# Start-up of a gated SSM and GELU-MLP kernel: warm-up matmuls on a constant, and one joint transpose of the state and bias rows behind the transposes of x

## The chip, the cores and the metric

The kernel runs on 1 core of one Trainium2 chip. The metric is the device time of one execution in microseconds (us). A run executes a kernel several times; the text quotes medians with the lowest and highest. The profile's span, from the first to the last instruction, is 1.7 to 2.2 us shorter than the time of the same execution.

## The reference, cut to what matters

```python
x = A_x                                     # 1 x 2048 x 640, bf16
g = sigmoid((x * gate_w).sum(-1))
a = S5 scan over 2048 steps: Bu = x @ B_bar.T ; h = Lam_bar * h + Bu ; y = 2 Re(h @ C.T) + x * Dskip
b = gelu(x @ w1 + b1) @ w2 + b2             # 640 -> 1728 -> 640
out = g * a + (1 - g) * b
```

`Lam_bar` and `B_bar` come from three vectors of 640 values (`Lambda_re`, `Lambda_im`, `log_dt`). For the argument only the beginning matters: the first 512 rows of x are transposed on TensorE, multiplied with W1 (five blocks of 128 input columns, k = 0 to 4, and seven column blocks of the output, jf = 0 to 6: 35 matmuls), and meanwhile the three state vectors and the bias b1, which arrive as rows, are transposed into columns.

## The kernel before

A small list scheduler, written in Python, orders the operations of each engine by priority and estimated duration when the program is built. Each engine then runs its own list in order, waiting on semaphores. `op(name, engine, duration, reads, writes, fn, prio)` is how an operation enters it.

```python
# loads: SP queue                                   (cut: B, C, W2, later x)
for h in range(2):                                  # first 512 rows of x in two halves, 320 KB each
    load(f"x0_{h}", "sp", ..., xn[0][:, 2 * h:2 * h + 2, :], x2[h * 256:(h + 1) * 256, :]..., prio=h)
for k in range(KD):                                 # W1, columns 0:896, 224 KB each
    load(f"w1_{k}", "sp", ..., W1sb[:, k, 0:FW], B_w1[k * 128:(k + 1) * 128, 0:FW], [("w1", k)], prio=2 + k)
# loads: ACT queue: three state vectors, the bias b1 in three pieces (behind a POOL memset of b1rows)

wz = SB("wz", [128, 512], BF16)                     # cleared by VectorE
def f_warm():
    for _ in range(6):
        t = nc.tensor.matmul(PS[6][:, :], wz[:, 0:128], wz[:, :], start=True, stop=True)
op("warm", "pe", 2.4, ["wz"], [("bank", 6)], f_warm, prio=-1000)

# TensorE, in the order in which the scheduler puts it:
#   six warm-ups | ten transposes of x, rows 0:256 | three transposes of the state rows ("cols")
#   | ten transposes of x, rows 256:512 | one filler matmul on wz | W1 matmuls k = 0, k = 1
#   | transpose of the bias rows ("colb") | W1 matmuls k = 2, 3, 4 | ...
# VectorE: copy of the state columns, five copies PSUM -> xT (k = 0..4), scan tables, ..., copy of the bias columns

for k in range(KD):                                 # first W1 matmuls, accumulating in banks 0 to 6
    for jf in ((5, 6, 0, 1, 2, 3, 4) if k == 0 else range(NW)):
        matmul(PS[jf], W1sb[:, k, jf * 128:(jf + 1) * 128], xT[:, k, 0:512], start=(k == 0), stop=(k == KD - 1))
```

The x transposes use banks 0 to 4, so W1 matmuls 5 and 6 can start as soon as xT block 0 is copied, and those of banks 0 to 4 need their bank's copy.

Of the kernel before, what the change touches and what calls it, by code (L numbers as in the profile page):

```python
# [8 lines left out]
FP32 = mybir.dt.float32  # L9
BF16 = mybir.dt.bfloat16  # L10
# [137 lines left out]
class Prog:  # L148
# [8 lines left out]
    def op(self, name, eng, dur, reads, writes, fn, prio=None, lat=0.0, after=()):  # L157
        deps = {}
        for k in reads:
            for w in self.last_w.get(k, ()):  # L160
                deps[w.idx] = w
        for k in writes:
            for w in self.last_w.get(k, ()):
                deps[w.idx] = w
            for r in self.last_r.get(k, ()):
                deps[r.idx] = r
        for a in after:
            deps[a.idx] = a
        deps = list(deps.values())
        E = self.E  # L170

        def run(eg, deps=deps, eng=eng, fn=fn):
            E.wait(eng, *[d.done for d in deps])
            return fn()

        it = self.sch.add(name, eng, dur, deps, run, prio=prio, lat=lat)
        for k in writes:
            self.last_w[k] = [it]
            self.last_r[k] = []
        for k in reads:  # L180
            self.last_r.setdefault(k, []).append(it)
        return it


def bass_gated_mix__ssm_conv_s5__dense_activation_gelu__prompt_kernel(
# [18 lines left out]
    _, S, D = A_x.shape  # L204
    P = A_Lambda_re.shape[0]
    F = B_w1.shape[1]
    assert S % 512 == 0 and D % 128 == 0 and P == D
    KD = D // 128
    KP = P // 128
# [4 lines left out]
    NF = (F + 127) // 128  # L214
    FL = F - (NF - 1) * 128
# [10 lines left out]
    with ExitStack() as es, nc.Block() as block:  # L226

        def SB(name, shape, dt):
            return es.enter_context(nc.sbuf_tensor(name, list(shape), dt))

        xT = SB("xT", [128, KD, S], BF16)
        xn = [SB(f"xn_{i}", [128, 4, D], BF16) for i in range(2)]
# [5 lines left out]
        GlL = [SB(f"GlL_{i}", [65, 512], BF16) for i in range(3)]  # L238
        dsk = SB("dsk", [128, D], BF16)
        gwb = SB("gwb", [128, D], BF16)  # L240
        b1col = SB("b1col", [128, NF], FP32)
        rows = SB("rows", [KP, 3, 128], BF16)
        b1rows = SB("b1rows", [NF, 128], BF16)
        lcol = SB("lcol", [128, 3, KP], FP32)
        dtb = SB("dtb", [128, KP], BF16)
        acol = SB("acol", [128, KP], FP32)
        thcol = SB("thcol", [128, KP], FP32)
# [5 lines left out]
        ident = SB("ident", [128, 128], BF16)  # L253
# [33 lines left out]
        PS = [es.enter_context(nc.psum_tensor(f"ps{i}", [128, 512], FP32)) for i in range(8)]  # L287
# [17 lines left out]
        op = pr.op  # L305

        def inc(eng, ins):
            return E.inc(eng, ins, eng + "_s")

        def dma_inc(eng, ins, sem):  # L310
            SEM(sem)
            E.count.setdefault(sem, 0)
            ins.then_inc(sems[sem], 16)
            E.count[sem] += 16
            return (sem, E.count[sem])
# [11 lines left out]
        def load(name, eng, sem, dst, src, writes, prio, dur=0.5, lat=2.5, reads=(), **kw):  # L327
            def fn():
                return dma_inc(eng, engines[eng].dma_start(dst, src), sem)
            return op(name, eng, dur, reads, writes, fn, prio=prio, lat=lat)  # L330
# [22 lines left out]
        load("w1_r", "sp", "l_w1r", W1sb[:, :, FW:F], B_w1[:, FW:F].rearrange("(k p) f -> p k f", p=128), [("w1", "r")], prio=6.5, lat=6.0)  # L353
        nmain = (NF - 1) * 128

        def f_b1z():
            return inc("pool", nc.gpsimd.memset(b1rows[:, :], 0.0))

        op("b1z", "pool", 0.2, (), ["b1a", ("b1b", 0), ("b1b", 1)], f_b1z, prio=-50)
        for i, (nm, src) in enumerate((("lre", A_Lambda_re), ("lim", A_Lambda_im), ("ldt", A_log_dt))):  # L360
            load(nm, "act", "l_" + nm, rows[:, i, :], src.rearrange("(k p) -> k p", p=128), [("rows", i)], prio=-100 + i, dur=0.45)
        load("b1a", "act", "l_b1a", b1rows[0:NF - 1, :], B_b1[0:nmain].rearrange("(j p) -> j p", p=128), ["b1a"], prio=-97, dur=0.4, lat=2.5)
        for h in range(2):
            load(f"b1b{h}", "act", f"l_b1b{h}", b1rows[NF - 1:NF, h * 64:h * 64 + FL], B_b1[nmain:F].rearrange("(j p) -> j p", j=1), [("b1b", h)],
                 prio=-96 + h, dur=0.4, lat=2.5)


# [12 lines left out]

        op("const", "dve", 0.8, ["iota"], ["ident"], f_const, prio=-65)

        wz = SB("wz", [128, 512], BF16)

        def f_wz():
            return inc("dve", nc.vector.memset(wz[:, :], 0.0))  # L386

        op("wz", "dve", 0.35, (), ["wz"], f_wz, prio=-70)

        def f_warm():  # L390
            t = None
            for _ in range(6):
                t = nc.tensor.matmul(PS[6][:, :], wz[:, 0:128], wz[:, :], start=True, stop=True)  # L393
            return inc("pe", t)

        op("warm", "pe", 2.4, ["wz"], [("bank", 6)], f_warm, prio=-1000)

        def f_ones():
            t = None
# [6 lines left out]
        def filler(name, n, prio, deps):  # L406
            def fn():
                t = None
                for _ in range(n):
                    t = nc.tensor.matmul(PS[6][:, :], wz[:, 0:128], wz[:, :], start=True, stop=True)  # L410
                return inc("pe", t)
            op(name, "pe", n * 0.22, ["wz"] + deps, [("bank", 6)], fn, prio=prio)

        for h in range(2):
            for k in range(KD):
# [6 lines left out]
                    return inc("pe", t)  # L422

                op(f"tp{h}{k}", "pe", 0.13, [("xn", 0, h), "ident"], [("bank", k)], f_tp, prio=-900 + 20 * h + k)
        filler("fill", 1, -860, [("xn", 0, 1)])
        for k in range(KD):

            def f_tpe(k=k):
# [7 lines left out]
        psC = PS[7][:, :].bitcast(BF16)  # L436

        def f_cols():
            t = None
            for i in range(3):  # L440
                t = nc.tensor.transpose(psC[:, i * 8:i * 8 + KP], rows[:, i, :], ident[0:KP, 0:KP])  # L441
            return inc("pe", t)

        op("cols", "pe", 0.3, [("rows", 0), ("rows", 1), ("rows", 2), "ident"], [("bank", 7)], f_cols, prio=-870)

        def f_cols1():
            return inc("dve", nc.vector.tensor_copy(out=lcol[:, :, :], in_=psC[:, 0:24].rearrange("p (a k) -> p a k", a=3)[:, :, 0:KP]))

        op("cols1", "dve", 0.2, [("bank", 7)], ["lcol"], f_cols1, prio=-3000)
        psD = PS[7][:, :].bitcast(BF16)  # L450

        def f_colb():
            return inc("pe", nc.tensor.transpose(psD[:, 0:NF], b1rows[:, :], ident[0:NF, 0:NF]))  # L453

        op("colb", "pe", 0.1, ["b1a", ("b1b", 0), ("b1b", 1), "ident"], [("bank", 7)], f_colb, prio=14.5)

        def f_colb1():
            return inc("dve", nc.vector.tensor_copy(out=b1col[:, :], in_=psD[:, 0:NF]))

        op("colb1", "dve", 0.2, [("bank", 7)], ["b1col"], f_colb1, prio=-1000)  # L460

        def f_dt():
            return inc("act", nc.scalar.activation(dtb[:, :], lcol[:, 2, :], ACT.Exp))

# [496 lines left out]
```

## Time and profile before

| | before |
|---|---|
| time, median of 3 (low to high) | 217.87 us (217.17 to 218.08) |
| span of the profiled run | 215.4 us |
| TensorE busy | 211.7 us, 98% |
| VectorE busy | 191.8 us, 89% |
| first W1 matmul | 6.10 us |
| from there to the end of the span | 209.27 us |

From the page of the kernel before: span, and busy time of each engine with its share.

```profile
span 215.4 us, 3296 instructions
...
PE 211.7 (98%) x1289; PEld 124.0 (58%) x1289; DVE 191.8 (89%) x270; ACT 99.3 (46%) x169; POOL 4.8 (2%) x14
```

The chain of waits of the kernel before, in order of time, for the first 16 us. Columns: start in us, length in us, what the chain went through ("issue" is time in which nothing that the profile shows was waited for).

```profile
0.87 0.28 DVE wz L386
...
1.20 2.74 PE ps L393 x6
3.94 1.08 PE ps L421 x10
5.02 0.17 PE ps L441 x3
5.19 0.86 PE ps L421 x10
6.04 0.22 PE ps L410
6.26 3.04 PE ps L635 x14
9.30 0.11 PE ps L453
9.41 4.64 PE ps L635 x21
```

After the clearing of the warm-up tile, the start-up chain is all TensorE: warm-ups (L393) from 1.20, ten transposes of x (L421), the state rows (L441), ten more transposes, the filler (L410), the W1 matmuls (L635), the bias rows (L453). The matmul lines of the timeline (start, length, engine, line, operation, tile, shape, count, idle time before) show the same operations, and at which pace they run:

```profile
3.77 1.25 PE L421 MATMUL ps<-ident,xn 128*128 128x128 bf16 x10
...
5.12 0.93 PE L421 MATMUL ps<-ident,xn 128*128 128x128 bf16 x10
...
6.10 2.12 PE L635 MATMUL ps<-xT,W1sb 128*128 128x512 bf16 x9
```

Ten transposes take 1.25 us at half clock (starts 107 ns apart). In the second ten the starts become 56 ns apart at about 5.56 us, which is also where the trace's record of the full clock begins. The semaphore events of the loads in this trace say: first half of x landed at 3.72, second half at 4.56, the first W1 tile at 5.94, only 0.16 us ahead of the first W1 matmul.

### The profile page before, as it was taken

The page shows a single profiled execution, that of the slowest core. Times are in us where ns is not written, and L with a number is a line of the kernel's source. Part 1 is how long each engine was busy: PE and PEld are TensorE (multiplying, and loading weights), DVE is VectorE, ACT ScalarE, POOL GpSimd, SP SyncE. Part 2 cuts the span into 40 slices and gives each one's busy share as a digit, 9 for nine tenths or more (in the row PEclk, how much of TensorE's full clock was granted, in tenths as well). Part 3 has the DMA queues.
Part 4 walks back from the last instruction along what each step waited for, and adds up shares of the span by engine and source line. Part 5 has one row for each costly group of instructions (what it writes and reads, how often), then busy time and mean ns, then how long its engine had stood idle before and what let it go on. Part 6 is the DMA issues. An engine that isn't in the chain of part 4 may idle for free.

```text
span 215.4 us, 3296 instructions
## 1 busy us (share of the span) xinstructions
PE 211.7 (98%) x1289; PEld 124.0 (58%) x1289; DVE 191.8 (89%) x270; ACT 99.3 (46%) x169; POOL 4.8 (2%) x14
## 2 busy tenths in 40 slices
PE   7999999999999999999999999999999999999995
PEld 3444444444577775444457777544457777777774
DVE  4899999999999999999996999799999999996313
ACT  2668556675432224556653323556662233232220
POOL 1010030000000100000000010000000000000000
PEclk9999999999999999999999999999999999999999
DMA  6998479996600230000000013000000000001001
GB/s 203 345 164 122 82 195 329 247 167 128 126 4 30 43 141 2 30 0 0 3 0 0 33 39 145 30 3 0 0 0 3 7 35 22 30 30 33 30 30 30
DMA packets 28201, 15.44 MB, mean 72 GB/s; under 512 B 22044, under 2 KB 27740, under 8 KB 28188
## 3 DMA queue, kind: packets, MB, share of 16 engines
q1 hardware_dynamic: 27568, 12.95, 24.4%
q0 software_dynamic: 560, 2.30, 3.4%
q8 instruction: 10, 0.16, 0.3%
q14 instruction: 3, 0.02, 0.0%
q10 hardware_dynamic: 60, 0.01, 0.0%
HBM read 7.38 MB, written 2.62 MB: 46 GB/s over the span
## 4 chain that ended last, share of the span: by engine, by line
PE 98%; DVE 0%; issue 0%
PE ps L774 26%; PE ps L654 23%; PE ps L800 20%; PE ps L699 20%; PE ps L635 4%; PE ps L775 2%; PE ps L393 1%; PE ps L675 1%; PE ps L421 1%; DVE osb L833 0%; DVE wz L386 0%; PE ps L410 0%; PE ps L441 0%; PE ps L453 0%
## 5 line engine op out<-in xcount | busy, mean ns | idle before, releaser
L774 PE MATMUL ps<-W2sb,Gl 128*128 128x320 bf16 x416 | 61.4, 299 | 0.0
L774 PEld LDWEIGHTS ps<-W2sb,Gl 128*128 128x128 bf16 x416 | 40.6, 98 | 16.6 <-issue 0.4
L654 PE MATMUL ps<-xT,W1sb 128*128 128x512 bf16 x225 | 49.2, 379 | 0.0
L800 PE MATMUL ps<-CT,H 128*128 128x320 bf16 (+2 forms) x330 | 46.1, 295 | 0.0
L739 DVE TENSOR_TENSOR_SCAN W<-atab,V 128x1280 bf16<-128x1280 f32 x16 | 44.3, 2811 | 0.3
L699 PE MATMUL ps<-xT,BT 128*128 128x512 bf16 x200 | 43.8, 379 | 0.0
L800 PEld LDWEIGHTS ps<-CT,H 128*128 128x128 bf16 x330 | 31.7, 98 | 12.0
L662 ACT ACTIVATE Gl<-ps,b1col 128x512 bf16<-128x512 f32 x45 | 30.6, 692 | 16.1 <-PE ps L654 16.1
L654 PEld LDWEIGHTS ps<-xT,W1sb 128*128 128x128 bf16 x225 | 22.1, 98 | 26.5
L699 PEld LDWEIGHTS ps<-xT,BT 128*128 128x128 bf16 x200 | 19.5, 98 | 23.4 <-issue 0.4
L708 ACT ACTIVATE U<-ps 128x512 bf16<-128x512 f32 x40 | 23.9, 597 | 18.3 <-PE ps L699 18.3
L819 DVE SCALAR_TENSOR_TENSOR xg<-xn,gcol,dsk 128x640 bf16<-128x640 bf16 x16 | 13.9, 882 | 0.4
L782 ACT ACTIVATE E_0<-ps,g1col 128x320 bf16<-128x320 f32 x12 | 6.3, 528 | 16.5 <-PE ps L775 16.5
L614 DVE SCALAR_TENSOR_TENSOR scr<-xn,gwb 128x640 bf16<-128x640 bf16 x16 | 13.2, 823 | 0.4
L503 DVE TENSOR_TENSOR V<-V,W 128x1280 bf16<-128x1280 bf16 x16 | 12.5, 821 | 0.3
L503 DVE TENSOR_TENSOR H<-H,V 128x1280 bf16<-128x1280 bf16 x16 | 12.5, 821 | 0.3
L503 DVE TENSOR_TENSOR V<-mr,U 128x2560 bf16<-128x2560 bf16 x8 | 11.9, 1489 | 0.5 <-DVE s L503 0.2
L503 DVE TENSOR_TENSOR H<-c,W 128x2560 bf16<-128x2560 bf16 x8 | 11.9, 1488 | 0.1
L503 DVE TENSOR_TENSOR V<-s,W 128x2560 bf16<-128x2560 bf16 x8 | 11.9, 1484 | 0.0
L503 DVE TENSOR_TENSOR W<-mi,U 128x2560 bf16<-128x2560 bf16 x8 | 11.9, 1484 | 0.0
L782 ACT ACTIVATE E_2<-ps,g1col 128x320 bf16<-128x320 f32 x10 | 5.3, 527 | 13.6 <-PE ps L775 13.6
L782 ACT ACTIVATE E_1<-ps,g1col 128x320 bf16<-128x320 f32 x10 | 5.3, 527 | 12.9 <-PE ps L775 12.9
(96 smaller groups left out, 124.8 us busy)
## 6 DMA issues: line engine op xcount, KB each, us to landing
out_dram<-osb SPq DMA_DIRECT2D x15, 160.0 KB, 1.8
W2sb<-in_B_w_dram SPq DMA_DIRECT2D x1, 2080.0 KB, 12.6
xn<-in_A_x_dram POOLq DMA_DIRECT2D x3, 640.0 KB, 4.8
W1sb<-in_B_w_dram SPq DMA_DIRECT2D x5, 224.0 KB, 4.3
W1sb<-in_B_w_dram SPq DMA_DIRECT2D x1, 1040.0 KB, 7.2
xn<-in_A_x_dram SPq DMA_DIRECT2D x2, 320.0 KB, 3.1
xT<-in_A_x_dram SPq DMA_TRANSPOSE x10, 4.3
dsk<-in_A_Dskip_dram POOLq DMA_DIRECT2D x1, 160.0 KB, 7.1
```

Source lines behind the costliest of these rows:

```text
L503: return inc("dve", nc.vector.tensor_tensor(out=o, in0=a, in1=b, op=o_))
L614: t = inc("dve", nc.vector.scalar_tensor_tensor(out=scr[:, :], in0=xn[q % 2][:, c, :], scalar=1.0, in1=gwb[:, :], op0=ALU.mult, op1=ALU.mu ...
L635: return inc("pe", nc.tensor.matmul(PS[jf][:, :], W1sb[:, k, jf * 128:(jf + 1) * 128], xT[:, k, 0:512], start=(k == 0), stop=(k == KD - 1)))
L654: t = nc.tensor.matmul(PS[bank][:, :], W1sb[:, k, jf * 128:(jf + 1) * 128], xT[:, k, q * 512:(q + 1) * 512], start=(k == 0), stop=(k == KD ...
L662: return inc("act", nc.scalar.activation(Gl[q % 2][:, jf, :], PS[bank][:, :], ACT.Gelu_apprx_tanh, bias=b1col[:, jf:jf + 1]))
L699: t = nc.tensor.matmul(PS[bank][:, :], BT[:, kd, ci, k * 128:(k + 1) * 128], xT[:, kd, q * 512:(q + 1) * 512], start=(kd == 0), stop=(kd = ...
L708: return inc("act", nc.scalar.activation(dst, src, ACT.Copy, scale=1.0 if ci == 0 else -1.0))
L739: t = inc("dve", nc.vector.tensor_tensor_scan(out=g[:, ci, :], data0=a, data1=v[:, ci, :], initial=0.0, op0=ALU.mult, op1=ALU.add))
L774: t = nc.tensor.matmul(PS[bank][:, 0:HALF], Gl[q % 2][:, jf, ts], W2sb[:, jf, cols], start=(jf == 0), stop=False)
L782: return inc("act", nc.scalar.activation(E1[c % NE][:, cols], PS[bank][:, 0:HALF], ACT.Copy, scale=g1col[:, c:c + 1]))
L800: t = nc.tensor.matmul(PS[bank][:, 0:n], H[b % NHB][:, ci, k, s * 128:(s + 1) * 128], CT[:, k, ci, cols], start=(i == 0), stop=(i == 2 * K ...
L819: return inc("dve", nc.vector.scalar_tensor_tensor(out=xg[c % 2][:, :], in0=xn[q % 2][:, c % 4, :], scalar=gcol[:, c:c + 1], in1=dsk[:, :] ...
```

## The change

Its intent: start the warm-ups earlier, with one more of them (no tile to clear first: they read a constant zero that the preamble writes, broadcast along the free dimension), so that the full clock comes earlier; and take work off TensorE's and VectorE's start-up: state rows and bias rows in one tile, one transpose instead of four, one copy instead of two, placed behind the transposes of x; no filler.

```diff
-        b1col = SB("b1col", [128, NF], FP32)
-        rows = SB("rows", [KP, 3, 128], BF16)
-        b1rows = SB("b1rows", [NF, 128], BF16)
-        lcol = SB("lcol", [128, 3, KP], FP32)
+        NR = 3 * KP + NF
+        rows = SB("rows", [NR, 128], BF16)
+        cols = SB("cols", [128, NR], FP32)
+        lcol = cols[:, 0:3 * KP].rearrange("p (a k) -> p a k", a=3)
+        b1col = cols[:, 3 * KP:NR]
...      (the loads write into rows; the memset of b1rows goes)
-        wz = SB("wz", [128, 512], BF16)
-        op("wz", "dve", 0.35, (), ["wz"], f_wz, prio=-70)
+        zero = nc.const_aps.tensor(0.0, [128, 512], FP32).bitcast(BF16)[:, :, 0]
...
-            for _ in range(6):
-                t = nc.tensor.matmul(PS[6][:, :], wz[:, 0:128], wz[:, :], start=True, stop=True)
+            for _ in range(7):
+                t = nc.tensor.matmul(PS[6][:, :], zero[:, 0:128], zero[:, :], start=True, stop=True)
...
-        filler("fill", 1, -860, [("xn", 0, 1)])
...
-        op("cols", "pe", 0.3, [("rows", 0), ("rows", 1), ("rows", 2), "ident"], [("bank", 7)], f_cols, prio=-870)
+            return inc("pe", nc.tensor.transpose(psC[:, 0:NR], rows[:, :], ident[0:NR, 0:NR]))
+        op("cols", "pe", 0.2, [("rows", 0), ("rows", 1), ("rows", 2), "b1a", ("b1b", 0), ("b1b", 1), "ident"], [("bank", 7)], f_cols, prio=-855)
...
-        op("colb", "pe", 0.1, [...], [("bank", 7)], f_colb, prio=14.5)
-        op("colb1", "dve", 0.2, [("bank", 7)], ["b1col"], f_colb1, prio=-1000)
+            return inc("dve", nc.vector.tensor_copy(out=cols[:, :], in_=psC[:, 0:NR]))
+        op("cols1", "dve", 0.2, [("bank", 7)], ["lcol", "b1col"], f_cols1, prio=-3000)
```

In the built program the joint transpose stands after the second W1 matmul, and its copy between the third and the fourth of the five xT copies.

More of the change, by code (lines that the diff above doesn't have):

```diff
@@ L354, in bass_gated_mix__ssm_conv_s5__dense_activation_gelu__prompt_kernel @@
         nmain = (NF - 1) * 128
-        def f_b1z():
-            return inc("pool", nc.gpsimd.memset(b1rows[:, :], 0.0))
-        op("b1z", "pool", 0.2, (), ["b1a", ("b1b", 0), ("b1b", 1)], f_b1z, prio=-50)
         for i, (nm, src) in enumerate((("lre", A_Lambda_re), ("lim", A_Lambda_im), ("ldt", A_log_dt))):
-            load(nm, "act", "l_" + nm, rows[:, i, :], src.rearrange("(k p) -> k p", p=128), [("rows", i)], prio=-100 + i, dur=0.45)
-        load("b1a", "act", "l_b1a", b1rows[0:NF - 1, :], B_b1[0:nmain].rearrange("(j p) -> j p", p=128), ["b1a"], prio=-97, dur=0.4, lat=2.5)
+            load(nm, "act", "l_" + nm, rows[i * KP:(i + 1) * KP, :], src.rearrange("(k p) -> k p", p=128), [("rows", i)], prio=-100 + i, dur=0.45)
+        load("b1a", "act", "l_b1a", rows[3 * KP:NR - 1, :], B_b1[0:nmain].rearrange("(j p) -> j p", p=128), ["b1a"], prio=-97, dur=0.4, lat=2.5)
         for h in range(2):
-            load(f"b1b{h}", "act", f"l_b1b{h}", b1rows[NF - 1:NF, h * 64:h * 64 + FL], B_b1[nmain:F].rearrange("(j p) -> j p", j=1), [("b1b", h)],
+            load(f"b1b{h}", "act", f"l_b1b{h}", rows[NR - 1:NR, h * 64:h * 64 + FL], B_b1[nmain:F].rearrange("(j p) -> j p", j=1), [("b1b", h)],
                  prio=-96 + h, dur=0.4, lat=2.5)
@@ L381, in bass_gated_mix__ssm_conv_s5__dense_activation_gelu__prompt_kernel @@
         op("const", "dve", 0.8, ["iota"], ["ident"], f_const, prio=-65)
-        wz = SB("wz", [128, 512], BF16)
-        def f_wz():
-            return inc("dve", nc.vector.memset(wz[:, :], 0.0))
-        op("wz", "dve", 0.35, (), ["wz"], f_wz, prio=-70)
+        zero = nc.const_aps.tensor(0.0, [128, 512], FP32).bitcast(BF16)[:, :, 0]
         def f_warm():
             t = None
-            for _ in range(6):
-                t = nc.tensor.matmul(PS[6][:, :], wz[:, 0:128], wz[:, :], start=True, stop=True)
+            for _ in range(7):
+                t = nc.tensor.matmul(PS[6][:, :], zero[:, 0:128], zero[:, :], start=True, stop=True)
             return inc("pe", t)
-        op("warm", "pe", 2.4, ["wz"], [("bank", 6)], f_warm, prio=-1000)
+        op("warm", "pe", 3.0, (), [("bank", 6)], f_warm, prio=-1000)
         def f_ones():
@@ L409, in fn @@
                 for _ in range(n):
-                    t = nc.tensor.matmul(PS[6][:, :], wz[:, 0:128], wz[:, :], start=True, stop=True)
+                    t = nc.tensor.matmul(PS[6][:, :], zero[:, 0:128], zero[:, :], start=True, stop=True)
                 return inc("pe", t)
-            op(name, "pe", n * 0.22, ["wz"] + deps, [("bank", 6)], fn, prio=prio)
+            op(name, "pe", n * 0.22, deps, [("bank", 6)], fn, prio=prio)
         for h in range(2):
@@ L438, in f_cols @@
         def f_cols():
-            t = None
-            for i in range(3):
-                t = nc.tensor.transpose(psC[:, i * 8:i * 8 + KP], rows[:, i, :], ident[0:KP, 0:KP])
-            return inc("pe", t)
-        op("cols", "pe", 0.3, [("rows", 0), ("rows", 1), ("rows", 2), "ident"], [("bank", 7)], f_cols, prio=-870)
-        def f_cols1():
-            return inc("dve", nc.vector.tensor_copy(out=lcol[:, :, :], in_=psC[:, 0:24].rearrange("p (a k) -> p a k", a=3)[:, :, 0:KP]))
-        op("cols1", "dve", 0.2, [("bank", 7)], ["lcol"], f_cols1, prio=-3000)
-        psD = PS[7][:, :].bitcast(BF16)
-        def f_colb():
-            return inc("pe", nc.tensor.transpose(psD[:, 0:NF], b1rows[:, :], ident[0:NF, 0:NF]))
-        op("colb", "pe", 0.1, ["b1a", ("b1b", 0), ("b1b", 1), "ident"], [("bank", 7)], f_colb, prio=14.5)
-        def f_colb1():
-            return inc("dve", nc.vector.tensor_copy(out=b1col[:, :], in_=psD[:, 0:NF]))
-        op("colb1", "dve", 0.2, [("bank", 7)], ["b1col"], f_colb1, prio=-1000)
+            return inc("pe", nc.tensor.transpose(psC[:, 0:NR], rows[:, :], ident[0:NR, 0:NR]))
+        op("cols", "pe", 0.2, [("rows", 0), ("rows", 1), ("rows", 2), "b1a", ("b1b", 0), ("b1b", 1), "ident"], [("bank", 7)], f_cols, prio=-855)
+        def f_cols1():
+            return inc("dve", nc.vector.tensor_copy(out=cols[:, :], in_=psC[:, 0:NR]))
+        op("cols1", "dve", 0.2, [("bank", 7)], ["lcol", "b1col"], f_cols1, prio=-3000)
         def f_dt():
```

## The prediction

> **What bounds the kernel.** TensorE: the page has PE busy 211.7 of 215.4 us, and the chain of waits is 98% PE. In the trace's single instructions no gap between matmul starts after 9.4 us exceeds 0.32 us. So about 206 us from the first W1 matmul on is fixed; only the time before it (6.10 us) and interruptions in the first 35 W1 matmuls can move. VectorE is 89% busy, but its H tiles are ready some 3 us early or more.
>
> **Start-up, from the timeline of before.** VectorE clears the warm-up tile at 0.87–1.14; six warm-ups start at 1.20 and, 427 ns apart, stream to 3.74. The first half of x lands at 3.72, the first ten transposes start at 3.77, 107 ns apart. Three transposes of the state rows run at 4.95–5.03; the second ten start at 5.12, although the second half of x landed at 4.56. Spacing falls from 107 to 55 ns at about 5.56: full clock, 4.36 us after the first warm-up. First copy of xT 5.55–5.98; filler 5.88; first W1 matmul 6.10. Its weights landed at 5.94, its xT copy ended at 5.98: both limits nearly coincide.
>
> **What the change does.**
> 1. Warm-ups start at about 0.75 instead of 1.20 (no memset to wait for). Seven last 2.99 us, to 3.74 again: x is not delayed. Full clock should come up to 0.45 us sooner.
> 2. The state rows leave the place between the halves: the second ten start at about 4.83, the first xT copy at about 5.26 instead of 5.55.
> 3. The filler (216 ns) goes. Still the first W1 matmul waits for its weights (5.94): about 6.02 instead of 6.10. Gain only 0.07 us in this profile.
> 4. The bias transpose cost PE 0.205 us (start to start 8.92 to 9.34, less 216 ns). The joint transpose after the second W1 matmul should cost about the same: no gain.
> 5. Loss: the joint copy (0.17 us) stands in VectorE's queue after three of five xT copies, and waits for the joint transpose (about 6.75). The last two copies come about 0.3 us late, and hold W1 matmuls six and seven, which need those banks: 0.1–0.2 us.
>
> For the profiled phase the sum is −0.07 + 0.15, about +0.1 us. But the Trainium skill, "TensorE: Matmul & The Clock Gate", section "Part 1: The HAM clock gate", says the activity window runs freely, so the moment of full clock varies from run to run. The unprofiled times spread over 217.17 to 218.08, profiled run 217.37; I take the slow ones as late clocks. Then, estimated from this trace's spacings, removing a half-rate filler gives 0.43 us, the earlier transposes 0.29, an earlier clock up to 0.22, less the losses: −0.5 to −0.8 us. Mixed: −0.4 us.
>
> **Prediction: 217.5 us, range 216.9 to 218.0. Faster by over 2% 0.01, within 2% 0.98, slower 0.01.**
>
> **What would show it.** First warm-up near 0.75 (1); second ten near 4.83 (2); first W1 matmul within 0.1 us of its weights' landing (3); a start-to-start gap near 0.4 us at the joint transpose (4); W1 matmul six or seven waiting on the copy (5); first W1 matmul to the end unchanged within 0.3 us.
>
> **What would make it wrong.** Full clock later than in before, by chance; constant operands read slower than the tile; the joint transpose waiting for a late bias load (5.65 in before); weights landing earlier than profiled, so that the earlier transposes pay fully.

## The result

| | before | after |
|---|---|---|
| time, median of 6 (low to high) | 217.85 us (217.17 to 218.08) | 217.50 us (217.24 to 217.73) |
| span of the profiled run | 215.4 us | 215.8 us |
| first warm-up | 1.20 us | 0.79 us |
| second ten transposes of x start | 5.12 us | 4.79 us |
| first W1 tile landed | 5.94 us | 6.43 us |
| first W1 matmul | 6.10 us | 6.57 us |
| from there to the end of the span | 209.27 us | 209.26 us |

The ratio of the times is 0.9987, 95% interval 0.9972 to 1.0002. (A ratio is the mean time of one kernel's fast runs over the mean of the other's fast runs of the same rounds, so not quite the ratio of the medians quoted.) The time is the same within 2%, and the gain of about 0.3 us is not clear of zero. The profiled execution of the changed kernel is even one of its slower ones, 0.4 us longer than the profiled one of before. That makes it useful: it shows what varies.

The chain of waits of the changed kernel, same stretch:

```profile
1.25 0.45 SPq L330
...
1.76 4.67 DMA W1sb<-in_B_w_dram
6.43 0.14 issue
6.57 0.59 PE ps L611 x2
7.16 0.12 PE ps L430
7.28 7.23 PE ps L611 x33
```

The start-up chain is no longer TensorE. It is the issue of the loads and then 4.67 us from the issue of the first W1 tile to its landing at 6.43; 0.14 us later the first W1 matmul starts (L611). The timeline of its TensorE:

```profile
0.79 3.14 PE L385 MATMUL ps<-const-float32-0.0 128*128 128x512 bf16 x7 [0.79 <-PEq L922]
3.73 2.34 PE L413 MATMUL ps<-ident,xn 128*128 128x128 bf16 x20
6.57 0.59 PE L611 MATMUL ps<-xT,W1sb 128*128 128x512 bf16 x2 [0.51 <-DMA W1sb<-in_B_w_dram]
7.09 0.18 PE L430 MATMUL ps<-ident,rows 29*128 29x29 bf16 x1
7.21 2.12 PE L611 MATMUL ps<-xT,W1sb 128*128 128x512 bf16 x9
```

The warm-ups start 0.41 us earlier, the twenty transposes follow one another, all at half clock in this execution (2.34 us), and then TensorE is idle for 0.51 us for the weights. From the first W1 matmul on the two kernels are equal to 0.02 us: the joint transpose (L430) costs 0.209 us (0.425 between the starts of W1 matmuls two and three, less a usual 0.216), as much as the bias transpose did (0.205).

### The profile page after: what moved, and what is told of

Its sections match the earlier page's. It is cut to its first block, busy times and chain, and to the rows that moved or that the text cites. A ratio compares the mean times of both kernels' runs of the same rounds, so it can differ in the third digit from the quotient of the medians.

```text
span 215.8 us, 3288 instructions
## 1 busy us (share of the span) xinstructions
PE 212.0 (98%) x1286; PEld 124.2 (58%) x1286; DVE 191.4 (89%) x268; ACT 99.3 (46%) x169; POOL 4.6 (2%) x13
## 4 chain that ended last, share of the span: by engine, by line
PE 96%; DMA 2%; SPq 0%; DVE 0%; issue 0%
PE ps L750 26%; PE ps L630 23%; PE ps L776 20%; PE ps L675 20%; PE ps L611 4%; DMA W1sb<-in_B_w_dram 2%; PE ps L751 2%; PE ps L651 1%; SPq L330 0%; DVE osb L809 0%; PE ps L430 0%
## 5 line engine op out<-in xcount | busy, mean ns | idle before, releaser
L638 ACT ACTIVATE Gl<-ps,cols 128x512 bf16<-128x512 f32 x45 | 30.6, 692 | 16.1 <-PE ps L630 16.1
```

The lines of the kernel that those rows point to most:

```text
L638: return inc("act", nc.scalar.activation(Gl[q % 2][:, jf, :], PS[bank][:, :], ACT.Gelu_apprx_tanh, bias=b1col[:, jf:jf + 1]))
```

## The experiments

All times are compared with runs of the kernel before on the same chip. Two theories were to be told apart. Landing theory: the landings of x and of the first W1 tile set the first W1 matmul, and after it everything is fixed. Clock theory: the moment of full clock sets the time, as the prediction supposed for the slow runs. (The expectations call the first one weights or DMA theory too.)

### The changed kernel twice more, as a control

> The changed kernel once more, as the control of this batch: 217.3 to 217.7 us, ratio to before 0.997 to 1.000. Both theories (weights: the landing of the first W1 tile sets the start of the first W1 matmul; clock: the moment of full clock sets it) expect the same time. Its profile tells them apart: the weights theory expects the first W1 matmul within 0.15 us of the landing of the first W1 tile whatever the clock does; the clock theory expects it to move with the moment at which matmul spacing halves.

> The changed kernel as the control of this batch: 217.3 to 217.7 us, ratio to before 0.998 to 1.000. Landing theory: span minus first W1 matmul again 209.27 us, first W1 matmul at the later of the weights' landing plus 0.14 and the x second half's landing plus 0.85, whatever the moment of full clock.

Measured: 217.59 us (217.05 to 217.91), ratio 0.9994, interval 0.9976 to 1.0011; and 217.35 us (217.19 to 218.21), ratio 0.9994, interval 0.9973 to 1.0014. Together with the first result: three estimates of a gain of 0.06% to 0.13%, or 0.1 to 0.3 us, none clear of zero. The chain of waits of the first of these runs:

```profile
1.26 4.00 DMA xn<-in_A_x_dram
...
5.31 0.30 PE ps L413 x2
...
5.63 0.44 DVE xT L420
...
6.11 0.61 PE ps L611 x2
```

Here the second half of x landed late (5.26 us in this view), and two transposes, one xT copy and semaphores made the 0.85 us to the first W1 matmul, although full clock had come at 3.92. In the second control the weights bound again (landing 5.94, first W1 matmul 6.07), with full clock at 3.79. So in three executions of the same kernel the binding landing was the weights, x, the weights; and full clock at 3.79, 3.92 and later than 5.75 us made no difference that the landing doesn't explain. Both theories' times were the same; the profiles speak for the landings.

### Weights that need not be waited for

```diff
-  matmul(PS[jf][:, :], W1sb[:, k, jf * 128:(jf + 1) * 128], xT[:, k, 0:512], ...)          # reads ("w1", k)
+  matmul(PS[jf][:, :], xn[0][:, 0, 0:128] if k == 0 else W1sb[...], xT[:, k, 0:512], ...)  # k == 0 reads ("xn", 0, 0)
```

The result is wrong on purpose. Made once from the changed kernel and once from the kernel before.

> The changed kernel with the first seven W1 matmuls taking their weights from the first half of x, which has long landed (wrong result on purpose). Weights theory: the first of them then starts as soon as its xT copy is done, near 5.75 us in the trace instead of 6.57, and the time falls by 0.3 to 0.8 us to 216.7 to 217.2. Clock theory: the time stays within 0.2 us of the changed kernel.

> The kernel before with the same other weights for its first seven W1 matmuls (wrong result on purpose). Weights theory: it gains less than the changed kernel does, since its later transposes and its filler hold the first W1 matmul near 6.05 us anyway: 217.2 to 217.6, so that the change would be worth 0.3 to 0.6 us where the weights are not waited for, against 0.3 with them. Clock theory: no gain, and the same distance between the two kernels as with the true weights.

Measured: changed kernel with borrowed weights 216.95 us (216.69 to 217.49), ratio to before 0.9971, interval 0.9954 to 0.9988; kernel before with borrowed weights 217.29 us (216.96 to 217.65), 0.9982, interval 0.9965 to 1.0000. In the first, W1 tile 0 landed at 6.04, and the first W1 matmul was at 5.88:

```profile
5.07 0.73 PE L413 MATMUL ps<-ident,xn 128*128 128x128 bf16 x10 [0.23 <-DMA xn<-in_A_x_dram]
5.39 1.09 DVE L420 COPY xT<-ps 128x512 bf16<-128x512 bf16 x3 [2.40 <-PE ps L413]
...
5.88 0.60 PE L611 MATMUL ps<-xT,xn 128*128 128x512 bf16 x2
```

It now follows the second half of x (landed 5.03) at the same distance, 0.85 us. So the wait for the first W1 tile costs the changed kernel about 0.5 us (0.9971 against its own 0.9994; six executions each) and the kernel before about 0.4, with an interval that just reaches 1. Both times lie where the landing theory expected them. The slow executions went too: of the eleven of the kernel before in this batch six took longer than 217.65 us, the longest of the six with borrowed weights. Nothing in the clock was changed for that, so the clock theory, which expected no gain, fails here as an account of the slow runs.

The clock isn't without effect, though. In the profiled execution of the kernel before with borrowed weights the first W1 matmul is at 6.07, as late as with its own weights (6.10): there TensorE's chain sets it, and that runs at half clock until 5.52. From its first transpose to the first W1 matmul it takes 2.33 us; in the version with the warm-ups alone, below, where full clock came at 4.47, the same chain takes 1.83 us. The expectation that the change would be worth clearly more without that wait isn't shown: the two versions with borrowed weights are 0.11% apart, the true kernels in the same batch 0.06%, and both are within the noise.

### Small loads behind the first W1 tile

```diff
-  load(nm, "act", ..., rows[i * KP:(i + 1) * KP, :], ...)                        # and the three pieces of b1
+  load(nm, "act", ..., rows[i * KP:(i + 1) * KP, :], ..., reads=[("w1", 0)])     # issued after W1 tile 0 has landed
```

(The first GELUs also wait for the sines, so that no activation table is loaded twice.)

> The changed kernel with the six small loads of state and bias rows issued only after the first W1 tile has landed. In both traces so far 10 or 11 of the 16 parts of that tile land within 0.5 us and the other 5 or 6 up to 1.3 us later. If the small loads in the second queue hold those parts up: last part by 5.3 us, first W1 matmul near 5.8, time 216.7 to 217.2. Rival, the late parts have another cause: the last part still lands at 5.9 to 6.4 us and the time is that of the changed kernel or longer, because the tables and the first GELUs start later.

Measured, in four executions: 221.08 us (220.62 to 221.22), ratio 1.0153, interval 1.0133 to 1.0173. The last parts of W1 tile 0 still landed at 5.74 and 5.94 us. The suspicion that the small loads hold them up is not supported, and why a few of the 16 parts come late stays open. The loss is another story, told by TensorE's waits (engine, what, line, released by: us in total, times, longest):

```profile
PE ps L430 <- DMA rows<-in_B_b_dram: 2.8, 1, 2.8
PE ps L630 <- ACT Gl L619: 0.9, 1, 0.9
```

The last small load (128 bytes) was issued at 8.26 and landed only at 13.43 us, 5.2 us later, among the transposing loads of B that had been issued before it; the joint transpose stood in TensorE's queue and waited 2.8 us for it.

### One part of the change alone

```diff
# warm_only: the kernel before, with
-  wz memset; six warm-ups and the filler on wz
+  seven warm-ups and the filler on the constant
# rows_only: the changed kernel, with
-  seven warm-ups on the constant
+  wz memset; six warm-ups on wz
```

> The kernel before with only the warm-up part of the change (seven on the constant, no memset). DMA theory (the landings of x and of the first W1 tile, then the filler, set the first W1 matmul, and the rest of the span is fixed at 209.27 us): first W1 matmul at 6.05 to 6.5 us, full clock possibly before 5 us without any effect, time within 0.15 us of before, 217.5 to 217.8. Clock theory: this part carries the gain, 217.2 to 217.4.

> The changed kernel with the old warm-ups (six, on a cleared tile). DMA theory: what little gain there is comes from here, 217.3 to 217.7, first W1 matmul within 0.15 us of the later of the first W1 tile's landing and the first xT copy's end; span minus first W1 matmul 209.27 us. Clock theory: no gain over before.

Measured: warm-ups alone 217.29 us (217.11 to 217.91), 0.9981, interval 0.9966 to 0.9997; rows alone 217.26 us (216.86 to 218.12), 0.9979, interval 0.9960 to 0.9998. Each by itself measured a little better than the whole change did in any batch, and outside what the landing theory expected of the warm-ups alone (217.5 to 217.8); the clock theory's 217.2 to 217.4 contains it. By time these parts can't be ranked: the intervals all overlap. The profiles can be read, because in this batch's two profiled executions the weights came early (5.46 and 5.45 us). The chain of waits with the warm-ups alone:

```profile
0.75 3.21 DMA xn<-in_A_x_dram
...
4.01 0.93 PE ps L416 x10
4.94 0.16 PE ps L436 x3
5.10 0.66 PE ps L416 x10
5.76 0.22 PE ps L405
5.98 3.05 PE ps L630 x14
```

and with the rows alone:

```profile
0.74 3.20 DMA xn<-in_A_x_dram
...
4.00 1.16 PE ps L418 x12
...
5.18 0.43 DVE xT L425
...
5.66 0.61 PE ps L616 x2
```

With the same landings of x (3.96 and 3.95 for the first half, 4.81 and 4.79 for the second) and full clock at 4.47 and 4.66, the version that keeps the state rows and the filler has its first W1 matmul at 5.83, the one without them at 5.66. That is what the rows part is worth in this pair of executions, where the weights were early: 0.18 us. The version with the earlier warm-ups had full clock 0.20 us sooner here, to no effect on the start of the first ten transposes, which waited for x; it did shorten these ten a little (0.71 us from the first start to the tenth, against 0.81).

### No warm-ups

```diff
-  op("warm", "pe", 3.0, (), [("bank", 6)], f_warm, prio=-1000)
```

> The changed kernel without its seven warm-up matmuls. Landing theory: the warm-ups matter only if full clock would otherwise come after the first W1 matmul. Without them TensorE's activity begins at the transposes (3.8 us), full clock comes some 3.1 to 5 us later, at 7 to 9 us, and the W1 matmuls from about 6.2 until then run at 427 ns instead of 216: 0.4 to 1.4 us longer than the changed kernel, 217.9 to 219. Span minus first W1 matmul then exceeds 209.27 by that amount. Rival: the warm-ups do nothing (time within 0.2 us of the changed kernel).

Measured: 219.22 us (217.79 to 220.77), ratio 1.0075, interval 1.0039 to 1.0111: 1.6 us longer than before, a little above the expected range, and spread over 3 us. TensorE's timeline:

```profile
5.01 1.25 PE L405 MATMUL ps<-ident,xn 128*128 128x128 bf16 x10
6.05 1.06 PE L603 MATMUL ps<-xT,W1sb 128*128 128x512 bf16 x2
...
7.18 3.16 PE L603 MATMUL ps<-xT,W1sb 128*128 128x512 bf16 x11
```

The first W1 matmul is at 6.05, as early as ever, but the first two take 1.06 us instead of 0.59: full clock came at 8.46, and the span after the first W1 matmul is 210.35 us, 1.09 more than 209.26. So a late clock does cost time when it comes after the first W1 matmul. In none of the profiled executions with warm-ups, old or new, did it come that late.

### Attempts at a better version

Splitting the first W1 tile, so that the two column blocks used first (64 KB) land ahead, and loading the second half of x from the ACT queue at once:

```diff
-  load("w1_0", "sp", W1sb[:, 0, 0:896])
+  load("w1_0a", "sp", W1sb[:, 0, 640:896]); load("w1_0b", "sp", W1sb[:, 0, 0:640])
# split_twoq, in addition
-  load("x0_1", "sp", ...)
+  load("x0_1", "act", ..., prio=-200)
```

> The changed kernel with its first W1 tile loaded in two pieces, the two columns blocks that are used first (64 KB) ahead of the other five (160 KB); right result. DMA theory: the small piece lands some 0.4 us after the second half of x instead of 0.6 to 1.9, so the first W1 matmul starts when its xT copy is done, as with the borrowed weights (5.9 us): 216.8 to 217.3, unless the second piece, needed 0.65 us later, still comes after 6.4 us; then a gap appears before the third W1 matmul. Rival (start set by the transposes or the clock): time as the changed kernel, 217.4 to 217.6.

> The same with the second half of x issued at once from the second queue instead of 0.5 us later from the first. If the start is set by when the x bytes arrive, the second half lands up to 0.4 us earlier and the time falls a further 0.1 to 0.4 us, to 216.5 to 217.0. Rival: all loads share one limited rate and the first half of x or the weights come later by as much, or the small loads, now behind it, hold the joint transpose: no further gain, or a loss.

Measured: split 217.33 us (216.87 to 217.56), 0.9979, interval 0.9963 to 0.9995; with two queues 217.06 us (216.97 to 217.87), 0.9976, interval 0.9959 to 0.9993. Both medians lie just above what was expected of them (216.8 to 217.3 and 216.5 to 217.0). In the first version the first W1 matmul is at 5.70, 0.85 us after the second half of x (4.85), as expected. But the third W1 matmul waited for the second piece, which landed at 6.50, and the chain of waits goes through it:

```profile
2.27 4.23 DMA W1sb<-in_B_w_dram
...
6.54 7.30 PE ps L613 x33
```

With two queues the two halves of x landed at 4.42 and 4.80 instead of 4.00 and 4.85: the same bytes by the same time, in one execution of each. The Trainium skill, "DMA: Bandwidth & Descriptors", section "Rules for kernel authors", says that spreading loads over issuing engines for bandwidth doesn't help, since they share the same 16 DMA engines; this trace agrees. Both versions lie slightly below before, not apart from the parts alone in the same batch.

The second attempt loads x by columns, so that W1 can begin with 256 KB of x instead of 640 KB (262 and 655 thousand bytes):

```diff
-  x rows 0:256, x rows 256:512, W1 tiles 0, 1, 2, ...
+  x columns 0:256, W1 tile 0 in two pieces, W1 tile 1, x columns 256:640, W1 tiles 2, ...
-  twenty transposes of x before the first W1 matmul, banks 0 to 4
+  eight before it (banks 0, 1); eight, and four with the joint transpose, later, through bank 7; six warm-ups
```

> A version of the changed kernel meant to move the limit, right result: x is loaded by columns (256 columns of all 512 rows, then, after the first two W1 tiles, the other 384), so that the first two xT tiles need 262 KB instead of 655; the first W1 tile comes in two pieces; the other three xT tiles pass through bank 7 while W1 matmuls run; six warm-ups. Landing theory (first W1 matmul follows the later of the needed x bytes plus 0.85 us and the needed weights plus 0.14 us; the rest of the span is fixed at 209.27): x part lands near 3.2, weights near 4.2, first W1 matmul 4.3 to 5.0 instead of 5.7 to 6.6; of these 1.2 to 1.6 us some is given back, because full clock comes at 3.9 to 5.6 and nine more transposes and a wait for a copy now stand between W1 matmuls (0.3 to 0.8 us): 216.3 to 217.0 us. Rival (start-up is bound by something other than the landings): first W1 matmul still near 6, time 217.3 or more.

Measured: 217.53 us (217.12 to 218.24), ratio 0.9999, interval 0.9978 to 1.0019. The chain of waits:

```profile
1.80 4.01 DMA W1sb<-in_B_w_dram
...
5.85 2.21 PE ps L617 x9
8.06 0.46 PE ps L420 x8
...
8.55 0.70 DVE xT L428
9.25 0.14 issue
9.38 0.38 PE ps L420 x4
...
9.88 4.64 PE ps L617 x21
```

The first W1 matmul came at 4.87, in the range that the landing theory gave, 1.2 us earlier than in before. That is partly luck: x landed at 3.70 and not near 3.2, the weights at 3.87 and not near 4.2, and from x to the matmul it took 1.17 us and not 0.85, since four transposes at half clock stood before the first copy instead of two at full clock. All of it was given back, and 0.5 us more: from there to the end took 210.96 us instead of 209.26. The third W1 matmul waited for the second piece of weights (landed 5.81), twelve transposes (0.46 and 0.38, and the joint one another 0.12) now stand between W1 matmuls, and the last four and the matmuls behind them wait for a copy out of bank 7 (0.70). The first part of the expectation held, the sum did not.

The third attempt adds to the split tile half copies of xT, so that the part from the first rows of x is copied while the second rows are on their way:

```diff
-  tensor_copy(xT[:, k, 0:512], bank k)                       after all four transposes of block k
+  tensor_copy(xT[:, k, 0:256], ...) after the first two; tensor_copy(xT[:, k, 256:512], ...) after the others
```

> An attempt at a version that beats both kernels, right result: the changed kernel with the first W1 tile in two pieces (as in the run of that name) and each xT copy in two halves, so that the half from the first rows of x is copied while the second rows are still on their way. Landing theory: from the landing of the second half of x to the first W1 matmul there remain about 0.65 us instead of 0.85, so the first W1 matmul starts near 5.5 us (second half at 4.5 to 5.0) unless the weights come later; 0.2 to 0.4 us below the changed kernel of this batch, 216.9 to 217.3. Rival: the second piece of weights or the small state loads now set the pace and a gap opens behind the first two W1 matmuls: time as the changed kernel.

Measured: 217.53 us (216.67 to 218.03), 0.9989, interval 0.9964 to 1.0015, beside 217.35 for the changed kernel in the same batch: no gain. The second half of x had landed at 4.75, so by the expectation W1 could have begun near 5.4; but the last part of even the 64 KB piece of weights landed at 5.64, and the first W1 matmul followed at 5.77. The weights are not the only reason. TensorE's and VectorE's timelines:

```profile
3.92 1.92 PE L415 MATMUL ps<-ident,xn 128*128 128x128 bf16 x20
4.33 2.07 DVE L422 COPY xT<-ps 128x256 bf16<-128x256 bf16 x10 [1.34 <-PE ps L415]
```

The ten half copies start 0.20 us apart. The sixth of them is the first that can take rows from the second half of x (that half's transposes of blocks 1 to 4 start one after another, each about 0.15 us after the end of one of the copies two to five). It ended at 5.61, 0.86 us after that half had landed; in the split version with whole copies the first copy ended 0.79 us after it (5.64, with x at 4.85). The half copies did not shorten the path at all, and with earlier weights W1 would have begun near 5.66 (an estimate: the end of that copy plus the 0.05 us that pass in the other traces). No version tried is clearly better than the changed kernel.

### All profiled executions side by side

Moments in us from the traces' single instructions and semaphore events. "x" is the landing of the second half of x (with two queues, of the half that landed last; by columns, of the first 256 columns), "W1" that of the first piece of W1 needed; "rest" is span end minus first W1 matmul. In "after" the trace has no record of full clock; the transposes were at half clock up to 5.75, the first W1 matmuls at full clock.

| run | first warm-up | full clock | x | W1 | first W1 matmul | rest |
|---|---|---|---|---|---|---|
| before | 1.20 | 5.56 | 4.56 | 5.94 | 6.10 | 209.27 |
| before, borrowed weights | 1.20 | 5.52 | 4.53 | not needed | 6.07 | 209.27 |
| warm-ups alone | 0.78 | 4.47 | 4.81 | 5.46 | 5.83 | 209.26 |
| rows alone | 1.19 | 4.66 | 4.79 | 5.45 | 5.66 | 209.26 |
| after | 0.79 | between 5.75 and 6.57 | 4.51 | 6.43 | 6.57 | 209.26 |
| after, again | 0.78 | 3.92 | 5.26 | 5.90 | 6.11 | 209.27 |
| after, third | 0.78 | 3.79 | 4.66 | 5.94 | 6.07 | 209.25 |
| after, borrowed weights | 0.78 | 4.54 | 5.03 | not needed | 5.88 | 209.26 |
| small loads late | 0.78 | 4.93 | 5.19 | 5.94 | 6.08 | 213.21 |
| no warm-ups | none | 8.46 | 4.97 | 5.81 | 6.05 | 210.35 |
| split | 0.78 | 3.99 | 4.85 | 5.33 | 5.70 | 209.45 |
| split, two queues | 0.78 | 4.49 | 4.80 | 4.99 | 5.83 | 209.26 |
| x by columns | 0.78 | 4.32 | 3.70 | 3.87 | 4.87 | 210.96 |
| split, half copies | 0.78 | 4.15 | 4.75 | 5.64 | 5.77 | 209.46 |

In every version of the changed kernel with whole copies and both halves of x from one queue, the first W1 matmul is within 0.03 us of the later of W1 plus 0.14 and x plus 0.85; where the clock is still half, at the transposes without warm-ups, x takes 1.08. With half copies W1 plus 0.14 fits as well; the 0.2 us more of rest there is one wait for a late part of C at 61 us. With two queues it is 0.18 later than x plus 0.85, because TensorE had to take the half that landed at 4.42 first and was busy with it until 5.04. In the versions that keep the filler and the state rows, TensorE itself takes that place: 5.83 where x plus 0.85 is 5.66.

## Why the prediction was right or wrong

The time was right: 217.5 us predicted, 217.50 measured in the first comparison, 217.59 and 217.35 in the controls. That tests little: the range of 216.9 to 218.0 holds the kernel before (217.85) too, and two of the terms behind the number were wrong, so that the closeness is luck.

- Step 1, the warm-ups: predicted near 0.75 with an end that leaves x alone; measured 0.79. The first half of x had landed at 3.57 in this execution and the transposes started at 3.73, when the warm-ups were through: they held x up by some 0.1 us, which cost nothing, as the weights came much later. "Full clock should come up to 0.45 us sooner" can't be confirmed from single executions: it came 3.0 to 4.15 us after the first warm-up in eight of the nine profiled executions of versions with these seven warm-ups from 0.79, and over 4.96 us after it in the ninth, which has no record of it before 5.75.
- Step 2, second ten transposes near 4.83: right in the profiled run (4.79), where they follow the first ten. In the controls the landing of x set them: at 4.70 in the third execution, near the prediction by chance, and at 5.31 in the second, because x itself was late, which the prediction hadn't considered.
- Step 3, the first W1 matmul bound by its weights: right. It followed the landing by 0.14 us instead of "within 0.1 us". This is the heart of the matter: the operations that the change took off the chain had a DMA landing close behind them.
- Step 4, the joint transpose as dear as the bias transpose: right, 0.209 against 0.205 us.
- Step 5, a loss of 0.1 to 0.2 us by the late xT copies: wrong. There is no gap behind the joint transpose, and the rest of the span is 209.26 us as before. The scheduler, which knew the order of the copies, had put a matmul of the second W1 tile in the sixth place and so covered the wait; the order of the built program showed this, and the prediction hadn't looked at it. For the profiled phase the sum should have been −0.07 us.
- The mixing step, "I take the slow ones as late clocks", failed. The prediction's −0.5 to −0.8 us for slow runs rested on it. The slow runs of the kernel before went with the wait for the first W1 tile (six executions with borrowed weights, none above 217.65 us), and they did not go with the change: over all batches the slowest of the 18 executions of the changed kernel took 218.21 us, the slowest of the 50 of the kernel before 218.19. In every profiled execution with warm-ups that has a record of it, full clock had come before the first W1 matmul; in the one without, the equal rest of 209.26 us says the same. What differs between executions is when x (4.51 to 5.26) and the first whole W1 tile (5.45 to 6.43) land; the profiled slower run of the changed kernel, 217.73 us, is a late W1 tile. So the mixed −0.4 us came out near the first measured difference (−0.35) by a wrong term and by luck. The three ratios make it 0.1 to 0.3 us.

The Trainium skill, "TensorE: Matmul & The Clock Gate", section "Part 1: The HAM clock gate", says that the activity window runs freely, so that the moment of full clock varies with where in it the first matmul falls. The traces agree that it varies (3.79 to over 5.75 us with the same kernel), and the version without warm-ups shows the price of a late one: times spread over 3 us. What the page couldn't say is whether this kernel is exposed to it. With six warm-ups its W1 matmuls already weren't in the executions profiled; its transposes were, as long as TensorE's chain and not a landing set the first W1 matmul.

What stays open: whether the change gains anything at all beyond about 0.2 us; how much of it each part gives (the warm-ups alone, at 217.29 us, came out where the clock theory had them, and no run separates an earlier clock from early weights there); and why the landings vary by up to 1 us between executions. A dependence of the unprofiled slow runs on the landings is inferred from the profiled ones and from the runs with borrowed weights, not shown for each.

## What to carry to other kernels

When a chain of waits shows one engine throughout, look up how close behind each step the next landing is: work taken off the chain gains only the distance to it, here at most 0.16 us to the weights. A change in the order or size of the loads has to be judged against the whole phase that follows, not the first matmul alone: starting W1 1.2 us earlier gave it all back within 5 us. And a difference of 0.3 us can't be ranked by six times that scatter by 0.8 us; the moments in the traces show at least which wait ended last in the execution that was profiled.

## What the Trainium skill lacked or had wrong

- "TensorE: Matmul & The Clock Gate", "Part 1": it puts the transition around 4 us into sustained activity, within 0.5 us from run to run. Here the delay from the first warm-up to full clock was 3.0 us in one execution of the changed kernel and over 4.96 us in another. (The same section also reports 6, 11 or 14 slow matmuls for one kernel, which is a wider spread than its 0.5 us.)
- The same page, "Part 4: PE-mode transpose", says that the full clock doesn't engage for transposes. Here transposes ran with starts 107 ns apart at half clock and 56 ns apart at full clock (ten in 1.25 and in 0.73 us).
- "DMA: Bandwidth & Descriptors", "Why a DMA increments its semaphore by 16 and not by 1": it says that the engines finish independently, but not how far apart. The 16 parts of one 224-KB load landed over 0.5 us in one execution and 1.5 us in another (4.96 to 6.43); the matmul waits for the last.
- No page has how long a small load takes behind transposing loads: 128 bytes, issued at 8.26 us, landed at 13.43.
- No page says what warm-up matmuls on a broadcast constant cost: starts 427 ns apart, as on a cleared tile.
